# Fillers from the first q piece, a cast load for block 0 of v, and its copies moved to ScalarE in a fused attention and channel-mix kernel

## The chip, the cores and the metric

The kernel runs on one core of a Trainium2 chip. The metric is device time in microseconds (us), as the median of several executions; less is better. PE is TensorE, DVE is VectorE, ACT is ScalarE, POOL is GpSimd; SP issues DMAs. Times on a timeline count from the start of the span. "L148" is line 148 of the kernel that the line is from; the changed kernel's numbers differ by a few. "Warm" and "cold" stand for PE at full and at half pace.

## The reference, cut to what matters

```python
# q, k, v: (4, 6208, 256) fp32
qn = q / (norm(q, axis=1) + 1e-6);  kn = k / (norm(k, axis=1) + 1e-6)
s = kn.transpose(0, 2, 1) @ qn / tau            # (4, 256, 256)
a = softmax(s, axis=-1)
x = v @ a
# channel mix of x with its rows shifted by one
xk = mu_k * x + (1 - mu_k) * x_prev;  xr = mu_r * x + (1 - mu_r) * x_prev
out = sigmoid(xr @ w_r) * (relu(xk @ w_k) ** 2 @ w_v)
```

A batch's `a` needs all rows of its q and k. So the kernel first streams q and k of batch 0 (12.7 MB), finishes its softmax, and only then can start on v. From there it works block by block (512 rows), and does the q and k work of batches 1 to 3 beside the blocks of the batch before.

## The kernel before: the parts concerned

The first stage takes pieces of 512 rows, in the order q q q q q q q, then k and q in turn, then the remaining k. Each piece is loaded as fp32, cast by DVE and squared by ACT; PE adds up `k^T q` in one PSUM bank and the column sums of the squares (128x1 matmuls) in another.

```python
    def q_piece(g, last=False):
        rows, n = rows_of(g)
        f = head_load(q, 0, g, 0, n)                       # SP, fp32
        qt = pq.tile([P, S, C], BF16, name="qb", ...)
        nc.vector.tensor_copy(qt[:rows, :n], f[:rows, :n])
        sq = pq.tile([P, S, C], BF16, name="hsq", tag="hsq", bufs=5)
        nc.scalar.activation(sq[:rows, :n], f[:rows, :n], AF.Square)
        flush()                                            # norm matmuls of the piece before
        pend.append((nq_ps, "q", sq, rows, n, last))
    # ... k_piece: the same, and 8 matmuls of 128x256 into s_ps0
    def filler(n):                                         # work for PE whose result nobody reads
        f_ps = ps.tile([P, M], F32, name="f_ps", tag="v", bufs=2)
        for u in range(n):
            nc.tensor.matmul(f_ps, ident, qb[0]...[:, :M], start=u == 0, stop=u == n - 1)
    # ... in the loop over pieces, after a k piece:
            if g == NB - 3:
                nc.scalar.copy(rq_bc0, bc_ps)              # the q norm, broadcast to all rows
            # ...
            if g == NB - 3:
                nc.gpsimd.tensor_copy(gate, kt[:, 0, 0:1]) # holds POOL until this k piece is cast
                nc.gpsimd.dma_start(w_k_sb, ...)           # cast loads, fp32 to bf16
                v_load(1)
                nc.gpsimd.dma_start(w_r_sb, ...)
                nc.gpsimd.dma_start(w_v_sb, ...)
```

After the last k piece comes the seam: block 0 of v by two plain loads and a cast on ACT, root and reciprocal of the k norm, exp, the scaled `a_sb`, the transposed block 0, the first mixed rows `xk` and the first up-projection `kT_ps`. After that PE is nearly always busy until the end.

Of the kernel before, what the change touches and what calls it, by code (L numbers as in the profile page):

```python
# [10 lines left out]
F32 = mybir.dt.float32  # L11
BF16 = mybir.dt.bfloat16
AX = mybir.AxisListType.X
AF = mybir.ActivationFunctionType
OP = mybir.AluOpType
# [3 lines left out]
def kernel(  # L19
# [13 lines left out]
    nc = tc.nc  # L33
    B, N, C = q.shape
    D = C
    DF = moe_w_k.shape[1]
    P = 128
    M = 512
    S = M // P
    assert C == 256 and DF == 1024  # L40
    NB = N // M
# [9 lines left out]
    pq = ctx.enter_context(tc.tile_pool(name="pq", bufs=4))  # L51
# [6 lines left out]
    ident = const.tile([P, P], BF16, name="ident")  # L58
# [16 lines left out]
    w_v_sb = const.tile([P, 8, D], BF16, name="w_v_sb")  # L75
    w_r_sb = const.tile([P, 2, D], BF16, name="w_r_sb")
    a_sb = const.tile([P, B, 2, C], BF16, name="a_sb")
    rq_bc0 = const.tile([P, C], F32, name="rq_bc0")
# [7 lines left out]
    def rows_of(g):  # L86
        return (P, S) if g < NB else (L, 1)


    qb = {}  # L90
    hk = {}
    NF = 8
    LEAD = 6
    F1, F2, F3 = 8, 2, 4
    NPE = 4

    def head_load(t, b, g, s0, s1):
        rows = rows_of(g)[0]
        f = pq.tile([P, S, C], F32, name="f", tag="f4", bufs=NF)
        nc.sync.dma_start(f[:rows, :s1 - s0], src_rows(t, b, g, s0, s1))  # L100
        return f
# [3 lines left out]
    s_ps0 = ps.tile([P, 2, C], F32, name="s_ps", tag="s")  # L105
    started = set()

    def first(key):
        if key in started:
            return False  # L110
        started.add(key)
        return True
# [9 lines left out]
    def flush():  # L122

        while pend:
            norm_mm(*pend.pop(0))

    def q_piece(g, last=False):
        rows, n = rows_of(g)
        f = head_load(q, 0, g, 0, n)
        qt = pq.tile([P, S, C], BF16, name="qb", tag="b2", bufs=NB + 1)  # L130
        qb[g] = qt
        nc.vector.tensor_copy(qt[:rows, :n], f[:rows, :n])
        sq = pq.tile([P, S, C], BF16, name="hsq", tag="hsq", bufs=5)
        nc.scalar.activation(sq[:rows, :n], f[:rows, :n], AF.Square)
        flush()
        pend.append((nq_ps, "q", sq, rows, n, last))

    def k_piece(g, s0, s1, last=False):
        rows, n = rows_of(g)
        n = s1 - s0  # L140
        f = head_load(k, 0, g, s0, s1)
        kt = pq.tile([P, S, C], BF16, name="kb", tag="kb", bufs=4)
        nc.vector.tensor_copy(kt[:rows, :n], f[:rows, :n])
        sq = pq.tile([P, S, C], BF16, name="hsq", tag="hsq", bufs=5)
        nc.scalar.activation(sq[:rows, :n], f[:rows, :n], AF.Square)
        for s in range(n):
            for ih in range(2):
                nc.tensor.matmul(s_ps0[:, ih, :], kt[:rows, s, ih * P:(ih + 1) * P], qb[g][:rows, s0 + s, :],  # L148
                                 start=first("s"), stop=last and s == n - 1, skip_group_check=True)
        flush()  # L150
        pend.append((nk_ps, "k", sq, rows, n, last))
        return kt

    def root(src, n):
        a = pn.tile([P, 4], F32, name="nrm_a")
        if len(src.shape) == 3:
            nc.vector.tensor_reduce(a[:, :n], src, axis=AX, op=OP.add)
        else:
            nc.vector.tensor_copy(a[:, :n], src)
        r = pn.tile([P, 4], F32, name="nrm_r")  # L160
        nc.gpsimd.tensor_tensor(r[:, :n], a[:, :n], half[:, :n], op=OP.pow)
        return r

    def inverse(r, n):

        nc.vector.tensor_scalar_add(r[:, :n], r[:, :n], 1e-6)
        o = pn.tile([P, 4], F32, name="nrm_o")
        nc.vector.reciprocal(o[:, :n], r[:, :n])
        return o


    def spread(r):
        dq = pn.tile([P, 2, P], F32, name="dq", bufs=1)
        for h in range(2):
            nc.vector.tensor_scalar_mul(dq[:, h], ident_f, r[:, h:h + 1])
        return dq

    def broadcast(dq, tag, **kw):
        bc_ps = ps.tile([P, C], F32, name="bc_ps", tag=tag, **kw)
        nc.tensor.matmul(bc_ps, ones_f, dq.rearrange("p h d -> p (h d)"), start=True, stop=True)  # L180
        return bc_ps

    def filler(n):

        f_ps = ps.tile([P, M], F32, name="f_ps", tag="v", bufs=2)
        for u in range(n):
            nc.tensor.matmul(f_ps, ident, qb[0].rearrange("p s c -> p (s c)")[:, :M], start=u == 0, stop=u == n - 1)

    def soft_half(b, ih, t_sb, rk, e_sb, sm, mx):

# [13 lines left out]
    def soft_tiles():  # L204
        return (pn.tile([P, 2, C], F32, name="t_sb"), pn.tile([P, 2, C], F32, name="e_sb"),
                pn.tile([P, 2], F32, name="sm"), pn.tile([P, 2], F32, name="mx"))
# [7 lines left out]
    st = {}  # L214
# [4 lines left out]
    def v_load(i):  # L219
        b, t = blocks[i]  # L220
        v_bf = pq.tile([P, S, C], BF16, name="v_bf", tag="b2", bufs=NB + 1)
        nc.gpsimd.dma_start(v_bf, v[b, t * M:(t + 1) * M, :].rearrange("(s p) c -> p s c", p=P))  # L222
        st[i, "v"] = v_bf

    def new_vT(i):

        vT = pq.tile([P, S, 2, P], BF16, name="vT", tag="b2", bufs=NB + 1)
        st[i, "vT"] = vT
        return vT
# [6 lines left out]
    def v_transpose_pe(i, v_bf, s0, s1, evac):  # L236
        vT = st[i, "vT"] if (i, "vT") in st else new_vT(i)
        n = s1 - s0
        vT_ps = ps.tile([P, S, 2, P], BF16, name="vT_ps", tag="kT", bufs=3)
        for s in range(n):  # L240
            for h in range(2):
                nc.tensor.transpose(vT_ps[:, s, h], v_bf[:, s0 + s, h * P:(h + 1) * P], ident)
        if evac == "v":
            nc.vector.tensor_copy(vT[:, s0:s1], vT_ps[:, :n])
        else:
            nc.scalar.copy(vT[:, s0:s1], vT_ps[:, :n])
# [263 lines left out]
    for what, g in order:  # L510
        if what == "q":
            q_piece(g, last=g == NB - 1)
        else:
            kt = k_piece(g, 0, rows_of(g)[1])
            if g == NB:
                nq = root(nq_ps, 2)
            if g == NB - LEAD + 1:
                bc_ps = broadcast(spread(inverse(nq, 2)), "v", bufs=2)
            if g == NB - 3:
                nc.scalar.copy(rq_bc0, bc_ps)  # L520
            if g == NB - 2:
                nc.sync.dma_start(mu_k_t, moe_mu_k.rearrange("(h p) -> p h", p=P))
                nc.sync.dma_start(mu_r_t, moe_mu_r.rearrange("(h p) -> p h", p=P))
            if g == NB - 3:
                nc.gpsimd.tensor_copy(gate, kt[:, 0, 0:1])
                nc.gpsimd.dma_start(w_k_sb, moe_w_k.rearrange("(ko ki) f -> ki ko f", ki=P))
                v_load(1)
                nc.gpsimd.dma_start(w_r_sb, moe_w_r.rearrange("(ko ki) d -> ki ko d", ki=P))
                nc.gpsimd.dma_start(w_v_sb, moe_w_v.rearrange("(fo fi) d -> fi fo d", fi=P))
    k_piece(NB - 1, 0, 2)  # L530
    k_piece(NB - 1, 2, 3)
    k_piece(NB - 1, 3, 4, last=True)
    flush()

    f0 = []
    for h in range(2):
        f = pq.tile([P, S, C], F32, name="f", tag="f4", bufs=NF)
        nc.sync.dma_start(f[:, :2], v[0, h * 256:(h + 1) * 256, :].rearrange("(s p) c -> p s c", p=P))
        f0.append(f)
    v0 = pq.tile([P, S, C], BF16, name="v_bf", tag="b2", bufs=NB + 1)  # L540
    for h in range(2):
        nc.scalar.copy(v0[:, 2 * h:2 * h + 2], f0[h][:, :2])

    t_sb, e_sb, sm, mx = soft_tiles()
    rk = root(nk_ps, 2)
    nc.vector.tensor_tensor(t_sb[:, 0], s_ps0[:, 0], rq_bc0, op=OP.mult)
    rk = inverse(rk, 2)
    if inv_tau != 1.0:
        nc.vector.tensor_scalar_mul(rk[:, 0:2], rk[:, 0:2], inv_tau)
    nc.vector.tensor_tensor(t_sb[:, 1], s_ps0[:, 1], rq_bc0, op=OP.mult)  # L550
    for ih in range(2):
        soft_half(0, ih, t_sb, rk, e_sb, sm, mx)
    nc.vector.tensor_scalar(omu, mu_k_t, -1.0, 1.0, op0=OP.mult, op1=OP.add)
    v_load(2)
    pos = {"load": 0}

# [7 lines left out]
    v_load(3)  # L564
    more_rows(3)
    v_load(4)
    for h in range(2):
        v_transpose_pe(0, v0, 2 * h, 2 * h + 2, "v")
    filler(F1)
    for ih in range(2):  # L570
        soft_scale(0, ih, e_sb, sm)

# [15 lines left out]
    for i in range(-2, NBLK):  # L588
        for j in range(8):
# [23 lines left out]
            n = i + 2  # L613
# [21 lines left out]
            if chain and (chain[0] is None or chain[0].__name__ != "bcast" or j in (3, 7)):  # L635
                f = chain.pop(0)
# [9 lines left out]
            for u in due.get(T, []):  # L646
                b, g, s = units[u]
# [48 lines left out]
```

## Time and profile before

| What | Value | Where from |
|---|---|---|
| time | 520.86 us (520.62 to 521.65, 4 runs) | timed runs |
| PE busy | 493.4 of 518.7 us, 95% | page, part 1 |
| last k piece lands | 37.0 us | DMA issues |
| k norm complete | 41.21 us | PE timeline, end of the last nk_ps matmul |
| first up-projection | 47.40 us | PE timeline |
| first full q, k group of batch 1 | lands 51.04, first used 53.45 us | DMA issues, PE timeline |

Read it from the end. PE bounds everything after about 52 us, so only the time up to the first up-projection can be won. The prediction shows the lines.

### The profile page before, as it was taken

What the parts mean: (1) busy time and instruction counts of PE and PEld (TensorE: products, weight loads), DVE (VectorE), ACT (ScalarE), POOL (GpSimd) and SP (SyncE); (2) the same over time, 40 slices, a digit from 0 to 9 for tenths busy, and PEclk for the clock granted to TensorE, in tenths of its full rate; (3) what the DMA queues carried; (4) which work ended last, traced back from release to release, by engine and by line L of the source; (5) the groups of instructions that cost most, each with busy time, mean ns of one, the idle gap of its engine ahead of it and who ended that gap; (6) DMA issues with size and microseconds to landing.
All of it is one profiled execution on the core that took longest, in us unless ns stands there. A gap on an engine that the chain in (4) does not pass through costs nothing. (4 is left out here: it accounts for less than half of the span.)

```text
span 518.7 us, 10189 instructions
## 1 busy us (share of the span) xinstructions
PE 493.4 (95%) x3730; PEld 340.5 (66%) x3730; DVE 451.6 (87%) x896; ACT 434.6 (84%) x831; POOL 102.9 (20%) x144
## 2 busy tenths in 40 slices
PE   1788999999999999999999999999999999999996
PEld 1564576676666667667666767667666666666675
DVE  3456899999999999999999999999988888888884
ACT  5776889998999899899999989899787777777773
POOL 0037432322251131131152123100031000000000
PEclk9999999999999999999999999999999999999999
DMA  8999999999999999699699999944298663432113
GB/s 309 407 329 185 193 204 193 196 204 186 132 185 219 164 169 171 117 175 170 108 168 220 167 170 168 157 114 85 61 163 147 128 117 87 102 83 80 57 66 102
DMA packets 143218, 83.77 MB, mean 161 GB/s; under 512 B 51200, under 2 KB 139840, under 8 KB 143168
## 3 DMA queue, kind: packets, MB, share of 16 engines
q0 software_dynamic: 65280, 32.74, 49.3%
q1 hardware_dynamic: 77728, 50.25, 39.2%
q8 instruction: 29, 0.48, 0.4%
q14 instruction: 21, 0.17, 0.1%
q10 hardware_dynamic: 160, 0.13, 0.1%
HBM read 78.71 MB, written 25.43 MB: 201 GB/s over the span
## 5 line engine op out<-in xcount | busy, mean ns | idle before, releaser
L337 ACT ACTIVATE kr<-kT_ps 128x512 bf16<-128x512 f32 (+1 forms) x392 | 232.4, 595 | 37.6 <-PE kT_ps L334 30.3
L334 PE MATMUL kT_ps<-xk,w_k_sb 128*128 128x512 bf16 (+1 forms) x784 | 231.6, 377 | 1.8 <-DVE xk L319 1.6
L382 PE MATMUL v_ps<-w_v_sb,kk 128*128 128x256 bf16 x1536 | 230.4, 273 | 0.0
L343 DVE TENSOR_TENSOR kk<-kr 128x512 bf16<-128x512 bf16 (+1 forms) x392 | 161.4, 416 | 35.8 <-ACT kr L337 32.2
L382 PEld LDWEIGHTS <-kk 128*128 128x128 bf16 x1536 | 150.2, 98 | 57.6
L425 ACT ACTIVATE sq<-qk 128x512 f32<-128x512 bf16 (+1 forms) x147 | 93.0, 633 | 0.0
L334 PEld LDWEIGHTS <-w_k_sb 128*128 128x128 bf16 x784 | 74.7, 98 | 22.4 <-issue 1.0
L353 PE MATMUL g_ps<-w_r_sb,xr 128*128 128x256 bf16 x388 | 73.8, 272 | 1.1 <-ACT ssq L462 1.1
L255 ACT CAST X<-xT_ps 128x512 bf16<-128x512 f32 x94 | 55.5, 590 | 20.8 <-PE xT_ps L253 20.0
L319 DVE SCALAR_TENSOR_TENSOR xr<-delta,mu_r_t,X 128x512 bf16<-128x512 bf16 x96 | 71.3, 743 | 0.0
L353 PEld LDWEIGHTS <-xr 128*128 128x128 bf16 x388 | 37.9, 98 | 48.9 <-issue 5.7
L319 DVE SCALAR_TENSOR_TENSOR xk<-delta,mu_k_t,X 128x512 bf16<-128x512 bf16 x94 | 69.9, 744 | 0.0
L395 DVE SCALAR_TENSOR_TENSOR res<-res,v_ps 128x512 f32<-128x512 f32 x96 | 65.2, 679 | 0.0
L411 POOL DMA_DIRECT2D qk<-in_q_dram x39 | 28.7, 736 | 170.4 <-ACT sq L425 167.0
L388 ACT ACTIVATE res<-g_ps 128x512 f32<-128x512 f32 x97 | 57.8, 596 | 0.4 <-PE g_ps L353 0.4
L253 PE MATMUL xT_ps<-vT,a_sb 128*128 128x512 bf16 x188 | 55.9, 379 | 0.2 <-ACT X L280 0.2
L421 PE MATMUL s_ps<-qk 128*128 128x256 bf16 (+1 forms) x294 | 56.1, 272 | 0.0
L222 POOL DMA_DIRECT2D v_bf<-in_v_dram x47 | 36.1, 774 | 51.4 <-DMA vT<-v_bf 46.7
L443 DVE TENSOR_TENSOR sq<-sq 128x1024 f32<-128x1024 f32 x36 | 43.8, 1218 | 1.0 <-ACT sq L425 1.0
L421 PEld LDWEIGHTS <-qk 128*128 128x128 bf16 (+1 forms) x294 | 26.7, 97 | 12.4 <-issue 1.3
L308 DVE TENSOR_TENSOR delta<-X 128x1024 bf16<-128x1024 bf16 x48 | 32.9, 685 | 0.1
L411 POOL DMA_DIRECT2D qk<-in_k_dram x39 | 29.0, 743 | 2.3 <-DMA qk<-in_q_dram 1.0
(73 smaller groups left out, 229.5 us busy)
## 6 DMA issues: line engine op xcount, KB each, us to landing
out_dram<-res SPq DMA_DIRECT2D x48, 512.0 KB, 3.4
v_bf<-in_v_dram POOLq DMA_DIRECT2D x47, 256.0 KB, 7.9
qk<-in_q_dram POOLq DMA_DIRECT2D x36, 256.0 KB, 6.6
qk<-in_k_dram POOLq DMA_DIRECT2D x36, 256.0 KB, 7.8
f<-in_q_dram SPq DMA_DIRECT2D x12, 512.0 KB, 8.6
f<-in_k_dram SPq DMA_DIRECT2D x11, 512.0 KB, 9.1
vT<-v_bf SPq DMA_TRANSPOSE x44, 6.5
f<-in_v_dram SPq DMA_DIRECT2D x2, 256.0 KB, 4.8
```

Source lines behind the costliest of these rows:

```text
L253: nc.tensor.matmul(xT_ps, a_sb[:, b, ih, dh * P:(dh + 1) * P], vT[:, :, ih, :], start=ih == 0, stop=ih == 1)
L319: nc.vector.scalar_tensor_tensor(o[:, dh], st[i, "d"][:, dh], mu[:, dh:dh + 1], X[:, dh, c:c + M], op0=OP.mult, op1=OP.add)
L334: nc.tensor.matmul(kT_ps[:, :m], w_k_sb[:, dh, fh * P:(fh + 1) * P], xk[:, dh, :m], start=dh == 0, stop=dh == 1)
L337: nc.scalar.activation(kr[:, :m], kT_ps[:, :m], AF.Relu, scale=RH)
L343: nc.vector.tensor_tensor(st[i, "kk"][:, fh, :m], kr[:, :m], kr[:, :m], op=OP.mult)
L353: nc.tensor.matmul(g_ps[:, s % 2], xr[:, dh, s * P:(s + 1) * P], w_r_sb[:, dh, :], start=s % 2 == 0 and dh == 0, stop=dh == 1, skip_group_ ...
L382: nc.tensor.matmul(v_ps[:, s % 2], kk[:, fh, s * P:(s + 1) * P], w_v_sb[:, fh, :], start=s % 2 == 0 and fh == 0, stop=fh == 7, skip_group_ ...
L388: nc.scalar.activation(st[i, "res"][:, 2 * u:2 * u + 2], st.pop((i, "g", u)), AF.Tanh, scale=0.5)
L395: nc.vector.scalar_tensor_tensor(r, r, 1.0, st.pop((i, "v", u)), op0=OP.add, op1=OP.mult)
L411: nc.gpsimd.dma_start(qk[:rows, :n, i], src_rows(t, b, g))
L421: nc.tensor.matmul(cov[b][:, ih, :], qk[:rows, s, 1, ih * P:(ih + 1) * P], qk[:rows, s, 0, :], start=g == GORD[0] and s == 0 and ih == 0, ...
L425: nc.scalar.activation(G["sq", s // 2][:rows, s % 2], qk[:rows, s], AF.Square)
```

## The change

The intent: keep PE busy from the start so that it runs at full pace when the last k pieces arrive; take ACT's wait for the q norm row away; spare ACT the cast of block 0; and free DVE in the seam. In the diff below, cuts are marked with "...".

```diff
-    F1, F2, F3 = 8, 2, 4
+    F1, F2, F3, FQ = 12, 2, 4, 3
...  in q_piece
         pend.append((nq_ps, "q", sq, rows, n, last))
+        if g < NB:
+            filler(FQ, g)
...  in k_piece
-        kt = pq.tile([P, S, C], BF16, name="kb", tag="kb", bufs=4)
+        kt = pq.tile([P, S, C], BF16, name="kb", tag="kb", bufs=6)
...  filler(n, src=0) reads qb[src] instead of qb[0]
-            if g == NB - 3:
-                nc.scalar.copy(rq_bc0, bc_ps)
+            if g == NB - 2:
+                nc.vector.tensor_copy(rq_bc0, bc_ps)
...
                 nc.gpsimd.tensor_copy(gate, kt[:, 0, 0:1])
+                v_load(0)
                 nc.gpsimd.dma_start(w_k_sb, ...)
                 v_load(1)
-                nc.gpsimd.dma_start(w_r_sb, ...)
-                nc.gpsimd.dma_start(w_v_sb, ...)
...  two plain loads of block 0 of v and their casts on ACT: taken out
+    v0 = st.pop((0, "v"))
+    for h in range(2):
+        v_transpose_pe(0, v0, 2 * h, 2 * h + 2, "s")      # copied from PSUM by ACT
+    filler(F1)
     for ih in range(2):
         soft_half(0, ih, t_sb, rk, e_sb, sm, mx)
...  both halves of t_sb are now made ahead of the reciprocal (one was behind it)
+    nc.gpsimd.dma_start(w_r_sb, ...)
+    nc.gpsimd.dma_start(w_v_sb, ...)
     v_load(2)
...
-    for h in range(2):
-        v_transpose_pe(0, v0, 2 * h, 2 * h + 2, "v")      # copied by DVE, after exp
-    filler(F1)
```

More of the change, by code (lines that the diff above doesn't have):

```diff
@@ L181, in broadcast, with filler @@
         return bc_ps
-    def filler(n):
+    def filler(n, src=0):
         f_ps = ps.tile([P, M], F32, name="f_ps", tag="v", bufs=2)
         for u in range(n):
-            nc.tensor.matmul(f_ps, ident, qb[0].rearrange("p s c -> p (s c)")[:, :M], start=u == 0, stop=u == n - 1)
+            nc.tensor.matmul(f_ps, ident, qb[src].rearrange("p s c -> p (s c)")[:, :M], start=u == 0, stop=u == n - 1)
     def soft_half(b, ih, t_sb, rk, e_sb, sm, mx):
@@ L525 @@
                 nc.gpsimd.tensor_copy(gate, kt[:, 0, 0:1])
+                v_load(0)
                 nc.gpsimd.dma_start(w_k_sb, moe_w_k.rearrange("(ko ki) f -> ki ko f", ki=P))
                 v_load(1)
-                nc.gpsimd.dma_start(w_r_sb, moe_w_r.rearrange("(ko ki) d -> ki ko d", ki=P))
-                nc.gpsimd.dma_start(w_v_sb, moe_w_v.rearrange("(fo fi) d -> fi fo d", fi=P))
     k_piece(NB - 1, 0, 2)
@@ L533 @@
     flush()
-    f0 = []
-    for h in range(2):
-        f = pq.tile([P, S, C], F32, name="f", tag="f4", bufs=NF)
-        nc.sync.dma_start(f[:, :2], v[0, h * 256:(h + 1) * 256, :].rearrange("(s p) c -> p s c", p=P))
-        f0.append(f)
-    v0 = pq.tile([P, S, C], BF16, name="v_bf", tag="b2", bufs=NB + 1)
-    for h in range(2):
-        nc.scalar.copy(v0[:, 2 * h:2 * h + 2], f0[h][:, :2])
     t_sb, e_sb, sm, mx = soft_tiles()
     rk = root(nk_ps, 2)
-    nc.vector.tensor_tensor(t_sb[:, 0], s_ps0[:, 0], rq_bc0, op=OP.mult)
+    for ih in range(2):
+        nc.vector.tensor_tensor(t_sb[:, ih], s_ps0[:, ih], rq_bc0, op=OP.mult)
     rk = inverse(rk, 2)
@@ L549 @@
         nc.vector.tensor_scalar_mul(rk[:, 0:2], rk[:, 0:2], inv_tau)
-    nc.vector.tensor_tensor(t_sb[:, 1], s_ps0[:, 1], rq_bc0, op=OP.mult)
+    v0 = st.pop((0, "v"))
+    for h in range(2):
+        v_transpose_pe(0, v0, 2 * h, 2 * h + 2, "s")
+    filler(F1)
     for ih in range(2):
@@ L553 @@
     nc.vector.tensor_scalar(omu, mu_k_t, -1.0, 1.0, op0=OP.mult, op1=OP.add)
+    nc.gpsimd.dma_start(w_r_sb, moe_w_r.rearrange("(ko ki) d -> ki ko d", ki=P))
+    nc.gpsimd.dma_start(w_v_sb, moe_w_v.rearrange("(fo fi) d -> fi fo d", fi=P))
     v_load(2)
@@ L566 @@
     v_load(4)
-    for h in range(2):
-        v_transpose_pe(0, v0, 2 * h, 2 * h + 2, "v")
-    filler(F1)
     for ih in range(2):
```

## The prediction

> **What bounds the kernel now.** I read the page first (parts 1 and 2), then the timelines of PE, ACT, DVE and POOL from 0 to 60 us, then the DMA issues of that stretch with their times to landing.
>
> ```profile
> PE 493.4 (95%) x3730; PEld 340.5 (66%) x3730; DVE 451.6 (87%) x896; ACT 434.6 (84%) x831; POOL 102.9 (20%) x144
> PE   1788999999999999999999999999999999999996
> ```
>
> From slice 5 on (about 52 us) PE is busy nine tenths or more and the change touches nothing there. So the change can only move the moment at which that PE-bound run starts. Before it lie two stages: about 37 us in which q and k of batch 0 stream in through fp32 tiles, and a "seam" of about 10 us (key norm, softmax, first v block, first mixed rows) up to the first up-projection, at 47.40 us. The seam, on the PE timeline:
>
> ```profile
> 32.26 1.89 PE L148 MATMUL s_ps<-qb,kb 128*128 128x256 bf16 x8 [0.87 <-DVE kb L143]
> 34.22 1.80 PE L148 MATMUL s_ps<-qb,kb 128*128 128x256 bf16 x8
> 36.06 0.68 PE L180 MATMUL bc_ps<-dq,ones_f 128*128 128x256 f32 x2
> 36.57 1.04 PE L148 MATMUL s_ps<-qb,kb 128*128 128x256 bf16 x8
> 37.65 1.03 PE L148 MATMUL s_ps<-qb,kb 128*128 128x256 bf16 x8
> ...
> 40.97 0.24 PE L117 MATMUL nk_ps<-ones_b,hsq 128*128 128x1 bf16 x4
> ...
> 45.00 0.39 PE L268 MATMUL xT_ps<-vT,a_sb 128*128 128x512 bf16 x1 [0.38 <-DVE a_sb L202]
> ...
> 47.40 0.85 PE L334 MATMUL kT_ps<-xk,w_k_sb 128*128 128x512 bf16 x2
> ```
>
> Columns: start, duration, engine, line, operation. The same eight matmuls take 1.89 us, then 1.04. Taking off one matmul (0.42 and 0.27 us) and dividing by 7 gives 0.21 and 0.11 us from start to start: PE is at half pace until about 36 us. From 32.26 on, no line of PE shows an idle wait until after 43 us: it works off a backlog. The last k piece lands at 37.0 us (issued at 31.55, 5.5 us to landing), yet the key norm is complete only at 41.21 (40.97 + 0.24). ACT loses time as well:
>
> ```profile
> 36.77 0.37 ACT L520 COPY rq_bc<-bc_ps 128x256 f32<-128x256 f32 x1 [1.56 <-PE bc_ps L180]
> 37.04 2.32 ACT L145 ACTIVATE hsq<-f 128x1024 bf16<-128x1024 f32 x4
> 39.27 1.12 ACT L542 CAST v_bf<-f 128x512 bf16<-128x512 f32 x2
> 42.64 0.51 ACT L197 ACTIVATE e_sb<-t_sb,nrm_o 128x256 f32<-128x256 f32 x1 [2.25 <-DVE nrm_o L168]
> ```
>
> It stands 1.56 us for the broadcast of the q norm, which waits its turn behind cold matmuls on PE, and the last four squares therefore end at 39.36.
>
> **What the Trainium skill says.** (1) "TensorE: Matmul & The Clock Gate", Part 1: the array idles at 1.2 GHz and goes to 2.4 GHz after about 3.4 us of sustained work; "Wait — 56ns, not 53.3ns?" there gives N / 1.2 GHz cold and N / 2.4 GHz + 2.5 ns warm, that is 213 and 109 ns for N = 256. The trace agrees on both paces, and PE had worked without a gap for 3.6 us (32.26 to about 35.85) when the pace changed. From 14 to 24 us PE had gaps of only 0.26 us in each 2.55 and stayed cold. The page's PEclk row shows 9 throughout and does not tell the two apart. (2) Same page, "Why this matters for your kernels": no idle gaps over about 3 us. Between 43.4 and 47.4 us gaps of 0.8 and 0.4 us left it warm. (3) "DMA: Bandwidth & Descriptors", "Issuing engines are not separate DMA queues": loads issued by SP and GpSimd share the same 16 engines. In the trace, cast loads move about 190 GB/s in bf16 bytes, which is 380 GB/s of fp32 read, against 400 to 420 for plain loads: a cast load is no cheaper on the engines, it only takes the cast off ACT.
>
> **The change, part by part.**
>
> *Fillers after each of 12 q pieces, 3 of N = 512.* Cold they cost 3 x 0.427 = 1.28 us (pace as above, scaled to 512), with the eight norm matmuls 0.37 us: 1.65 us of work per 1.28 us piece. PE saturates from about 6 us and should be warm by 10 to 13 us. Warm, a pair of a q and a k piece needs 7 x 0.11 + 0.27 = 1.04 (s) + about 0.55 (norms) + 0.65 (fillers) = 2.2 us per 2.55 us of loading, so there is no backlog. Fillers end with the last q piece (28.8 us); k pieces alone then cost about 1.07 us each (37.65 less 36.57) per 1.28 us, 80%, which I expect to keep PE warm. PE is not the bound there, so 36 fillers add nothing directly. The first stage stays bound by DMA: the last k piece still lands at 37.0.
>
> *q norm row copied by DVE, two pieces later.* Takes away ACT's 1.56 us wait and 0.27 us of copy (37.04 less 36.77). The square of k piece 10 starts at its landing, 35.55, and the four squares end at 35.55 + 2.32 = 37.9; DVE pays 0.37 us among its casts.
>
> *kb buffers 4 to 6.* Removes two DVE waits for PE (0.58 and 0.83 us before the last two casts), which a PE without backlog would have removed anyway.
>
> *Norm complete:* 37.9 + last four norm matmuls, about 0.35 = **38.3** instead of 41.21: 2.9 us earlier.
>
> *Chain from norm to exp.* Before: copy 41.24, power on POOL to 42.20, reciprocal to 42.6, exp at 42.64, that is 1.43 us after the norm. After: the same, 39.75, if ACT is free. But v of block 0 now comes by a cast load, issued behind the gate (k piece 9, 35.0 before), and its two transposed halves are copied on ACT ahead of exp. The first cast load's packets begin to move about 2 us after issue, as k ends; 256 KB at 190 GB/s is 1.35 us, so it lands at about 38.7. Transposes to 39.2, two ACT copies of about 0.55 us from 39.1: exp starts at about **40.3**, not 39.75. DVE, rid of the vT copies (0.75 us), then scales sooner: before, the second a_sb let PE go 2.36 us after exp began (45.00 less 42.64); I take 1.9. So xT at 42.2 against 45.00: **2.8 us** gained. F1 = 12 fillers (2.6 us from 39.2) end at 41.8, just before.
>
> *After it* the steps to the first up-projection are unchanged (2.4 us), so 44.6 instead of 47.40. Block 1 of v (landed 42.3) is needed at about 43.3, w_k (landed 40.95) at 44.6. w_r and w_v are issued later but fall in behind v1 in a queue that never empties; they are needed after 51. Load order and bytes are otherwise the same, so landings hardly move.
>
> Sum: 520.77 - 2.8 = **518.0 us**.
>
> **Rivals.** *(a) The cast load is the new bound.* v of block 0 gates both ACT copies and, through ACT's order, exp. For: its issue waits for the gate and the first packets of this queue are slow (171 GB/s from 36 to 38 us). Against: the estimate above leaves it 0.5 us late only. If it lands at 40 instead of 38.7, gain 1.5 us: 519.3. *(b) The loop becomes load-bound.* The first full q, k group lands at 51.04 (k part: issued 44.78, 6.3 us) and was first used at 53.45, a slack of 2.41 us, less than the 2.8 gained; the next groups have 5.6 us and more. So PE may wait 0.4 us once; but DVE is 97% busy from 48 to 58 and PE waits on it there anyway (0.60 us before 54.78), so I count 0.1 us. If it cascades: 519.5. *(c) PE stays or falls cold again* in the k-only stretch: the backlog returns and the norm is back at about 40.5 to 41; gain 0 to 0.7: 520.3. *(d) Nothing reaches the end.* A shift of the start under a PE bound passes through whole; I see no later stop.
>
> **Range and chances.** Centre 518.0; (a) to (c) all push up, a faster seam (exp not held by ACT) would give 517.4. Eight in ten: 517.0 to 519.9. Two per cent is 10.4 us, the whole seam: faster by that 0.01, slower 0.01, same 0.98.
>
> **What would show it.** s_ps groups of eight at 1.04 us from the first k piece on; ACT without the wait for bc_ps; last nk_ps matmul ending at 38.3; first v load landing at 38.7 and exp at 40.3; first kT at 44.6; PE's wait before the first full group under 0.5 us; PE busy time over the span about unchanged. The prediction is wrong if 8-matmul groups near 36 us still take 1.89, if exp waits on v well past 40.3, or if kT starts early but the end does not follow.

## The result, and the profile after

The changed kernel takes **518.88 us** (518.72 to 519.07, 4 runs) against 520.86: 2.0 us less. The ratio is 0.9960, 95% interval 0.9942 to 0.9977. A repeat later, in 5 rounds, gave 518.88 us again and a ratio of 0.9967 (0.9955 to 0.9979). That is within the range of 517.0 to 519.9, and short of the centre, 518.0, by 0.9 us.

The page of the changed kernel, parts 1 and 2:

```profile
PE 496.5 (96%) x3770; PEld 340.4 (66%) x3770; DVE 451.2 (87%) x895; ACT 434.7 (84%) x830; POOL 104.1 (20%) x145
PE   5789899999999999999999999999999999999996
```

The first slices of PE are fuller (5, 7, 8, 9 instead of 1, 7, 8, 8): those are the fillers. The fifth is emptier than its neighbours, 8; that is the new thing to explain. The PE timeline of the changed kernel (start, duration, engine, line, operation, count, and in brackets the idle time before it and what ended it):

```profile
6.16 1.44 PE L189 MATMUL f_ps<-qb,ident 128*128 128x512 bf16 x3 [2.56 <-DVE qb L132]
...
9.14 1.30 PE L189 MATMUL f_ps<-qb,ident 128*128 128x512 bf16 x3
...
10.48 0.81 PE L189 MATMUL f_ps<-qb,ident 128*128 128x512 bf16 x3
...
13.85 1.05 PE L150 MATMUL s_ps<-qb,kb 128*128 128x256 bf16 x8 [0.46 <-DVE kb L145]
...
31.80 1.05 PE L150 MATMUL s_ps<-qb,kb 128*128 128x256 bf16 x8 [0.87 <-DVE kb L145]
...
38.91 0.24 PE L117 MATMUL nk_ps<-ones_b,hsq 128*128 128x1 bf16 x4
39.58 0.62 PE L244 MATMUL vT_ps<-ident,v_bf 128*128 128x128 bf16 x8 [0.43 <-DMA v_bf<-in_v_dram]
...
42.63 0.59 PE L270 MATMUL xT_ps<-vT,a_sb 128*128 128x512 bf16 x2
...
45.48 0.60 PE L336 MATMUL kT_ps<-xk,w_k_sb 128*128 128x512 bf16 x2
...
50.54 0.39 PE L423 MATMUL s_ps<-qk 64*128 64x256 bf16 x2 [0.39 <-DMA qk<-in_k_dram]
...
53.21 0.39 PE L423 MATMUL s_ps<-qk 128*128 128x256 bf16 x2 [1.29 <-DMA qk<-in_k_dram]
```

Three fillers take 1.44 us at first and 0.81 us from 10.5 us on: PE has reached full pace, 25 us sooner than before, and in this trace every k group of eight matmuls takes 1.03 to 1.05 us. The k norm is complete at 39.15 us (38.91 + 0.24) instead of 41.21, and the first up-projection starts at 45.48 instead of 47.40: 1.92 us sooner. Then come two waits that the kernel before did not have. In the waits of PE between 46 and 150 us (who waited for whom: us in total, times, longest), the largest of each kernel are, before and then after:

```profile
PE kT_ps L334 <- DVE xk L319: 0.6, 1, 0.6
```
```profile
PE s_ps L423 <- DMA qk<-in_k_dram: 1.7, 2, 1.3
```

Lining up the up-projection matmuls of both traces one by one gives the gain along the way: 1.91 us at the first, 2.16 at the fifth, 0.35 at the seventeenth (just after the second wait), 1.30 at the nineteenth, and 1.25 at the last of 784. So about 0.9 us of the 2.16 was given back within 9 us, and the rest went through to the end unchanged. (In this pair of traces the spans differ by 1.4 us, 518.7 and 517.3; the timed medians by 2.0.)

ACT in the seam of the changed kernel:

```profile
35.49 2.19 ACT L147 ACTIVATE hsq<-f 128x1024 bf16<-128x1024 f32 x4 [0.30 <-DMA f<-in_k_dram]
40.01 1.07 ACT L248 COPY vT<-vT_ps 128x512 bf16<-128x512 bf16 x2 [2.33 <-PE vT_ps L244]
40.97 0.52 ACT L199 ACTIVATE e_sb<-t_sb,nrm_o 128x256 f32<-128x256 f32 x1
```

The wait for the q norm row is gone and the last squares end at 37.68 us. But exp (L199) starts at 40.97, right behind the two vT copies, and these waited 2.33 us for the transposes, which wait for block 0 of v: it lands at 39.53 us (issued 35.06, on its way for 4.5 us).

### The profile page after: what moved, and what is told of

The parts are those of the page before. It is cut to its first block, busy times and chain, and to the rows that moved or that the text cites. A ratio compares the mean times of both kernels' runs of the same rounds, so it can differ in the third digit from the quotient of the medians.

```text
span 517.3 us, 10260 instructions
## 1 busy us (share of the span) xinstructions
PE 496.5 (96%) x3770; PEld 340.4 (66%) x3770; DVE 451.2 (87%) x895; ACT 434.7 (84%) x830; POOL 104.1 (20%) x145
## 5 line engine op out<-in xcount | busy, mean ns | idle before, releaser
L355 PEld LDWEIGHTS <-xr 128*128 128x128 bf16 x388 | 37.9, 98 | 48.2 <-issue 4.8
L224 POOL DMA_DIRECT2D v_bf<-in_v_dram x48 | 37.3, 779 | 52.4 <-DMA vT<-v_bf 46.9
```

The lines of the kernel that those rows point to most:

```text
L355: nc.tensor.matmul(g_ps[:, s % 2], xr[:, dh, s * P:(s + 1) * P], w_r_sb[:, dh, :], start=s % 2 == 0 and dh == 0, stop=dh == 1, skip_group_ ...
```

## The experiments

Two questions were open. Which part of the change won the 2 us at the start? Theory A says the warm PE; its rival, the parts that relieve ACT and DVE. And what made the loop's loads late? Theory B says the cast load of block 0, theory C (formed after theory B's runs) that together with the late issue of w_r and w_v. Theory D, on what bounds the tail of k, came last. Twelve runs were made, two of them repeats, all correct, with 5 rounds each. For each, from its trace: the end of the last nk_ps matmul ("norm"), the start of the first up-projection ("up"), the landing of the first full q, k group of batch 1 ("group"), and PE's waits for qk in sum.

| Run | median us | ratio to before | norm | up | group | waits |
|---|---|---|---|---|---|---|
| before | 520.86 | 1 | 41.21 | 47.40 | 51.04 | 0 |
| changed | 518.88 | 0.9960 | 39.15 | 45.48 | 53.16 | 1.7 |
| no_fill | 521.90 | 1.0013 | 42.00 | 47.93 | 55.45 | 1.3 |
| fill_only | 518.61 | 0.9949 | 39.03 | 45.22 | 50.50 | 0 |
| v0_plain | 518.96 | 0.9955 | 39.17 | 45.11 | 52.92 | 1.6 |
| gate_early | 519.32 | 0.9968 | 39.37 | 45.62 | 53.40 | 1.8 |
| w_early | 518.60 | 0.9952 | 39.20 | 45.59 | 52.79 | 1.0 |
| loads_back | 518.01 | 0.9942 | 38.96 | 44.53 | 50.66 | 0 |
| fill_root | 518.41 | 0.9950 | 38.93 | 45.11 | 50.83 | 0 |
| fill_six | 520.97 | 1.0003 | 41.54 | 47.72 | 51.64 | 0 |
| after_again | 518.88 | 0.9967 | 39.24 | 45.74 | 53.15 | 1.3 |
| back_again | 517.81 | 0.9946 | 39.07 | 44.64 | 50.90 | 0 |
| back_kb4_rq | 517.69 | 0.9945 | 39.41 | 44.98 | 50.71 | 0 |
| loads_root | 517.62 | 0.9941 | 38.94 | 44.51 | 50.55 | 0 |

The ratios' intervals are about 0.0012 to either side (0.0018 for the first result); the last four columns come from one trace each, and the two traces of the changed kernel differ by 0.26 us in "up" and 0.4 us in the waits; "before" of the table is the first measurement, and each group of four had its own runs of it (medians 521.35, 521.18 and 520.76).

### no_fill and fill_only: the fillers alone

no_fill is the changed kernel without them; fill_only is the kernel before with nothing else.

```diff
 no_fill
-        if g < NB:
-            filler(FQ, g)
 fill_only (on the kernel before)
+        if g < NB:
+            filler(FQ, g)
```

> The changed kernel without the three fillers after each q piece. Theory A (warm PE shortens the tail of k): the s_ps groups of eight take 1.89 us again up to about 36 us, the last nk_ps matmul ends at 40.5 to 41.2 instead of 39.15, first kT at about 47, total 520.0 to 520.8 us. Rival (the copy on VectorE and the other v path did it, the fillers are idle work): nk_ps still ends before 39.5 and the total stays within 0.4 us of 518.9.

> The kernel before plus only the fillers of the q pieces (F1 stays 8, v by plain loads, q norm row copied on ScalarE). Theory A: nk_ps ends at about 39.2, first kT at about 45.5, and because the loads land as before (first full q, k group at 51.0) PE waits for it less than 0.5 us: total 518.5 to 519.0, as good as the whole change or better. Rival: 520.3 to 520.8.

The PE timeline of no_fill:

```profile
18.95 1.05 PE L148 MATMUL s_ps<-qb,kb 128*128 128x256 bf16 x8 [0.64 <-DVE kb L143]
...
21.50 1.89 PE L148 MATMUL s_ps<-qb,kb 128*128 128x256 bf16 x8 [1.13 <-DVE kb L143]
...
36.84 1.56 PE L148 MATMUL s_ps<-qb,kb 128*128 128x256 bf16 x8
...
41.76 0.24 PE L117 MATMUL nk_ps<-ones_b,hsq 128*128 128x1 bf16 x4
```

and that of fill_only, with ACT's copy of the q norm row last:

```profile
32.79 1.05 PE L150 MATMUL s_ps<-qb,kb 128*128 128x256 bf16 x8
...
38.79 0.24 PE L117 MATMUL nk_ps<-ones_b,hsq 128*128 128x1 bf16 x4
...
45.22 0.85 PE L336 MATMUL kT_ps<-xk,w_k_sb 128*128 128x512 bf16 x2
```
```profile
35.17 0.35 ACT L522 COPY rq_bc<-bc_ps 128x256 f32<-128x256 f32 x1
```

Without fillers the norm is complete at 42.00 us and nothing is gained; the total is even a little over the kernel before (521.90 against 521.35 in the same rounds). The norm, the first up-projection and the total all came later than expected. PE did reach full pace by itself, at 17.42 us, but fell back at 20.83 and stayed at half pace until 37.90 us, within the group at 36.84: about 2 us later than in the trace of the kernel before (35.80). With fillers alone it is complete at 39.03 us, the first up-projection starts 2.18 us sooner than before, and the lined-up gain is still 2.17 us at the last one: all of it arrives. So the fillers alone give the whole gain of the change; what its other parts win and lose comes below. fill_only's ACT also copies the q norm row without any wait (at 35.17, right behind the square before): ACT's 1.56 us of before were PE's slow pace, seen from ACT.

### fill_six: is it enough to warm PE up once?

```diff
 fill_six (on fill_only)
-        if g < NB:
+        if g < LEAD:            # LEAD = 6
             filler(FQ, g)
```

> Fillers alone on the kernel before, but only after the first six q pieces; none after 13 us. If fillers are needed only to warm PE and its own work (some 60 per cent of a q, k pair) holds it: s_ps groups of eight stay at 1.05 us throughout, total 518.6 as with all twelve. Rival (the own work lets it fall back as it never warmed it up): groups go back to 1.89 us before 30 us, total 520.3 to 521.

The PE timeline of fill_six:

```profile
21.51 1.05 PE L150 MATMUL s_ps<-qb,kb 128*128 128x256 bf16 x8 [1.13 <-DVE kb L145]
...
25.42 1.89 PE L150 MATMUL s_ps<-qb,kb 128*128 128x256 bf16 x8 [2.48 <-DVE kb L145]
```

The expectation fell, but not at once. PE's own work held the full pace through four k groups with idle waits of up to 1.18 us. The next group, after a wait of 2.48 us, is at half pace. There the loads paused: 2.5 us pass between two landings, 20.74 and 23.26, instead of the usual 1.28 (the kernel before has the same pause, 2.25 us from 21.04 on). The total, 520.97, is that of the kernel before.

That the long wait took the pace is not shown, though. Here is the busy time by stretch in fill_six (stretch; its length; busy us of PE, PEld, DVE, ACT and POOL; granted clock; DMA share; GB/s):

```profile
22.00:23.00 1.00, 0.94 (x22) 0.80 (x19) 0.00 (x0) 0.00 (x0) 0.00 (x0) 1.00 1.04 414
23.00:24.00 1.00, 0.00 (x0) 0.00 (x0) 0.69 (x1) 0.64 (x1) 0.00 (x0) 0.51 1.01 401
```

The granted clock fell at 23.03 us, when the wait had lasted 0.1 us. In no_fill it fell at 20.83, after a wait of 0.64 us and 0.5 us into one of 1.13. And three runs with all twelve groups of fillers lost the pace too, v0_plain at 22.87, loads_root at 23.14 and back_kb4_rq at 24.70 us, with waits of 1.73 to 1.95 us in the same pause of the loads. They had it back 3.4 us later, as v0_plain's PE timeline shows:

```profile
22.86 1.89 PE L150 MATMUL s_ps<-qb,kb 128*128 128x256 bf16 x8 [1.73 <-DVE kb L145]
...
26.25 1.06 PE L150 MATMUL s_ps<-qb,kb 128*128 128x256 bf16 x8
```

In each of these five traces the recorded changes before 40 us lie whole multiples of 3.41 us apart (3.41, 13.65 and 17.07 us). What decides at such a moment stays open: PE was busy for 43% (loads_root) to 68% (no_fill) of the 3.41 us before a fall, and for only 56% before a moment of fill_six, 16.20 us, without one. What the runs do show is the outcome. With twelve groups of fillers PE was at full pace from 28.2 us on in every trace, in time for the tail of k; without the last six it came back only at 36.68 us. The mean granted clock of the timed runs agrees: 0.994 or more in every run with twelve groups, 0.980 to 0.986 in all five of fill_six, and below 0.990 in 20 of the 31 runs of the kernel before that ran beside the experiments. By this, most runs of the kernel before reached full pace early and lost it again; its profiled run, at half pace until 35.80 us, is not typical in that.

### v0_plain, gate_early, w_early, loads_back: why the loads are late

In the changed kernel three things differ in the loads: block 0 of v goes through the cast queue, no plain load runs while that queue starts up, and w_r and w_v are issued only after the k norm.

```diff
 v0_plain   (on the changed kernel): block 0 of v by two plain loads on SP, cast on ACT
-                v_load(0)
+    # after the last k piece, as in the kernel before
 gate_early (on the changed kernel)
-            if g == NB - 3:
+            if g == NB - 4:
                 nc.gpsimd.tensor_copy(gate, kt[:, 0, 0:1])
 w_early    (on the changed kernel): w_r and w_v behind the gate again, no longer after the k norm
                 v_load(1)
+                nc.gpsimd.dma_start(w_r_sb, ...)
+                nc.gpsimd.dma_start(w_v_sb, ...)
 loads_back: v0_plain and w_early together
```

> The changed kernel, but block 0 of v comes as in the kernel before, by two plain fp32 loads on SP and a cast on ScalarE. Theory B (the cast load of v0 is what delays the later cast loads: it replaces a transfer that filled the DMA engines while the first cast load was being set up): the first full q, k group lands at about 51.0 to 51.5 instead of 53.16, PE's waits for qk fall from 1.7 us to under 0.7, total 517.9 to 518.3. Rival (the late issue of w_r and w_v delays them): the waits stay above 1.2 us and the total stays at 518.9.

> The changed kernel with the gate of the cast loads at the k piece before (NB - 4 instead of NB - 3), about 1.2 us earlier. Theory B: the DMA engines' hole between 35 and 37.5 us closes in part, v0 lands at about 38.3 instead of 39.53, the first full q, k group at about 52.0 instead of 53.16, PE's waits for qk fall to about 0.5 us, total 517.9 to 518.3. Rival (the early cast loads take bandwidth from the last k pieces): last k lands 0.5 to 1 us later than 36.77 and the total stays within 0.3 us of 518.9.

> The changed kernel with w_r and w_v issued again behind the gate, right after block 1 of v. Theory C (two holes in the DMA stream push the loop's loads back: one of 2 us before the first cast load, since no plain v load fills it, and one that comes of issuing w_r and w_v only after the key norm): the second hole goes and the first stays, the first full q, k group lands at 51.8 to 52.4 instead of 53.16, PE waits 0.7 to 1.3 us for it instead of 1.7, first kT stays at 45.5, total 518.2 to 518.6. Rival (only the first hole counts): still 53.1 and 518.9.

> The changed kernel with all its loads as in the kernel before: block 0 of v by two plain loads and a cast on ScalarE, w_r and w_v behind the gate. Fillers, 6 kb buffers, q norm row on VectorE, vT copied on ScalarE and 12 fillers in the seam stay. Theory C: first full q, k group lands at about 51, PE waits for it under 0.7 us, first kT gains 2.3 us and all or nearly all of it arrives at the end: total 518.3 to 518.7, the same as fillers alone within 0.3 us. Rival (something else in the new parts costs time in the loop): 518.9 or more.

The busy times by stretch, in the columns of above, tell where the DMA engines had little to do. First the changed kernel, then v0_plain, then loads_back:

```profile
36.00:38.00 2.00, 2.00 (x33) 1.82 (x32) 1.46 (x5) 1.68 (x4) 1.92 (x3) 1.00 0.37 49
42.00:44.00 2.00, 2.00 (x10) 0.76 (x8) 0.64 (x4) 0.76 (x2) 2.00 (x4) 1.00 1.40 192
```
```profile
36.00:38.00 2.00, 2.00 (x33) 1.82 (x32) 1.45 (x5) 2.00 (x5) 0.68 (x1) 1.00 0.85 156
42.00:44.00 2.00, 1.74 (x12) 0.75 (x11) 0.80 (x3) 0.69 (x2) 2.00 (x4) 1.00 0.83 97
```
```profile
36.00:38.00 2.00, 2.00 (x34) 1.82 (x32) 1.47 (x5) 2.00 (x5) 2.00 (x3) 1.00 1.07 166
42.00:44.00 2.00, 2.00 (x17) 1.15 (x16) 0.80 (x3) 1.26 (x2) 1.88 (x3) 1.00 1.45 202
```

In the changed kernel the engines move 49 GB/s from 36 to 38 us, since the k loads are done and the cast queue has only begun; with the plain loads of v they move 156. From 34 to 38 us the plain loads make up 0.5 MB, all of block 0 in fp32, in time that is otherwise lost; cast, the same block takes 256 KB / 190 GB/s = 1.4 us of the queue that everything later waits in. In v0_plain that hole is filled and another opens, 97 GB/s from 42 to 44 us: with less ahead of them, the late w_r and w_v now find the queue run dry. In loads_back neither is there, the first full group lands at 50.66, and PE does not wait.

Theory B fell with v0_plain: it expected the group by 51.5, waits under 0.7 and 518.3 us or less, and got 52.92, 1.6 and 518.96. Theory C had the two costs add up, and that part was wrong: w_early was expected to land the group by 52.4, and landed it at 52.79. Against loads_back (50.66) each of the two alone costs about 2 us at that group, both together 2.5. A likely reason is that a queue pushed back by the one still has work when the other's hole would come: in the changed kernel 192 GB/s move from 42 to 44 us. How much of the cast load's cost is the lost time and how much its own 1.4 us in the queue was not separated. gate_early, which was to close the first hole in part, missed too: the gate came only about 0.6 us sooner in this trace (issue at 34.44 instead of 35.06), v0 landed at 38.99, the last k piece was late by 0.27 us (37.04), and the second hole (120 GB/s from 43 to 44 us) ate the rest; 519.32 us is no better than the changed kernel.

loads_back is faster than both kernels, 518.01 us, and faster than was expected (518.3 to 518.7): its first up-projection starts 2.87 us sooner than before, not 2.3. Run again beside the changed kernel:

> The changed kernel once more, as the yardstick of the next three on the same chip: 518.7 to 519.2 us, PE's waits for qk 1.5 to 1.8 us in sum.

> The changed kernel with its loads as in the kernel before, once more beside the changed kernel. Theory C: 0.6 to 1.2 us faster than the changed kernel of the same rounds, ratios apart by 0.0012 to 0.0023. If the first result was chance: within 0.3 us.

517.81 against 518.88 us, ratios 0.9946 and 0.9967: 1.1 us, as expected (the changed kernel's waits were 1.3 us this time, under the expected 1.5 to 1.8). Its first up-projection starts at 44.53 us (44.64 in the repeat), 0.6 to 0.7 us ahead of fill_only's 45.22, though the norm ends within 0.1 us of it. That is what the rest of the change is worth in the seam, with the vT copies on ACT and DVE free to scale at once; its parts (these copies, 12 fillers instead of 8, the order of the t_sb products) were not tested apart. In the timed runs the difference of loads_back and fill_only (0.9946 or 0.9942 against 0.9949, in different rounds) is within the intervals, so it is seen in the traces alone.

### back_kb4_rq: the kb buffers and the q norm row

```diff
 back_kb4_rq (on loads_back)
-        kt = ... bufs=6
+        kt = ... bufs=4
-            if g == NB - 2:
-                nc.vector.tensor_copy(rq_bc0, bc_ps)
+            if g == NB - 3:
+                nc.scalar.copy(rq_bc0, bc_ps)
```

> The same with 4 kb buffers and the q norm row copied on ScalarE at its old place. If these two parts only removed waits that a warm PE removes anyway: within 0.3 us of that kernel, ScalarE's copy of 0.35 us without a wait of over 0.2 us, VectorE without waits for PE before its last casts. Rival (each is worth its wait of before, 1.56 us and 1.41 us): the last nk_ps matmul ends 0.5 us or more later and the total is 518.5 to 519.5.

517.69 against 517.81 us of the same rounds. ACT's copy takes 0.35 us without a wait, and DVE waits for PE before none of its last casts. The norm ends 0.34 us later than in back_again, inside what was allowed. The two parts, taken back together, buy nothing measurable: both waits were PE's pace.

### fill_root and loads_root: what bounds the tail of k now

In the warm runs so far DVE stands 1.3 to 1.5 us for the q norm before it casts k piece 6, already landed. These two take the norm one piece later.

```diff
 fill_root (on fill_only), loads_root (on loads_back)
-            if g == NB:
+            if g == NB - LEAD:
                 nq = root(nq_ps, 2)
```

> Fillers alone on the kernel before, and the root of the q norm taken one k piece later in VectorE's order, so that the cast of k piece 6, landed at 30.2 us, need not stand behind the wait for the q norm (1.33 us in the trace). Theory D (with a warm PE the tail of k is bound by PE from the first of its k pieces on, 31.7 us): PE starts that tail 0.7 us sooner, the last nk_ps matmul ends at 38.1 to 38.5 instead of 39.0, total 517.9 to 518.2 against 518.6 of fillers alone. Rival (ScalarE's squares or the landings bound the tail): unchanged within 0.3 us.

> The changed kernel with its loads as before and the root of the q norm one k piece later. The tail of k is then bound by the landings (fill_root ended nk_ps only 0.1 us sooner): within 0.3 us of the kernel without the moved root, and PE's first full group waits for its load up to 0.3 us. If PE's late start was the bound after all: 0.5 us faster.

In fill_root PE starts k piece 6 at 31.07 instead of 31.68 us, and yet the norm ends at 38.93 instead of 39.03: PE now waits for a cast of k piece 10 (0.20 us, before 36.43) and then runs without a gap:

```profile
36.43 1.05 PE L150 MATMUL s_ps<-qb,kb 128*128 128x256 bf16 x8 [0.20 <-DVE kb L145]
...
38.69 0.24 PE L117 MATMUL nk_ps<-ones_b,hsq 128*128 128x1 bf16 x4
```

Theory D fell (it expected the norm by 38.5 and 518.2 us or less; the total is 518.41). Its rival had the right size, within 0.3 us, but only half the reason: the landing and cast of piece 10 set the start, and what remains is PE's own work from there, 2.5 us from 36.43. loads_root, 517.62 us, is 0.2 us under back_again, within the noise, as expected; PE did not wait for its first full group. It is the fastest median by a hair; the simpler loads_back is as good within the intervals.

## Why the prediction was right or wrong

**Warm PE: right.** Predicted by 10 to 13 us, seen at about 10.3; k groups at 1.05 us from the first on; no backlog at the end of the q pieces. That fillers after the last q piece are not needed also held. In part this was luck: "I expect to keep PE warm" rested on 80% load (1.07 of 1.28 us is 84%), and neither the load nor the wait alone sorts the traces that lost the pace, with all fillers in three of them, from those that kept it.

**Norm complete at 38.3: too early by 0.85 us.** The failed step is "37.9 + last four norm matmuls, about 0.35". ACT's squares did end when predicted (37.68), but PE was not waiting for them: from 31.80 us it has no idle wait until 39.15, and 1.47 us of its own work was left when ACT was done. Six k pieces at 1.07 us, the last of them in three parts, and the broadcast, about 0.5 us, fill that time. I compared PE's 1.07 us with the 1.28 us of a landing and concluded that there was no backlog. I left out that after piece 10 is cast PE still has two pieces to do, 2.5 us in fill_root. That PE gets k piece 6 only at 31.80 (landed 30.2) adds little: fill_root starts it 0.6 us sooner and gains 0.1 us. Measured gain of this term 2.06 us, predicted 2.9.

**The 1.56 us of ACT and the kb waits: listed as gains of their own, not so.** The prediction said of the buffers that a warm PE would remove their waits anyway, and back_kb4_rq shows it; the same is true of ACT's wait, which the prediction booked to the copy on DVE. (The copy moved by one k piece, from NB - 3 to NB - 2, not by two as the prediction says.)

**v of block 0: right in kind.** Rival (a) was partly there: landing at 39.53 instead of 38.7, exp at 40.97 instead of 40.3. POOL spent 1.35 us on the first cast load's issue, and its first packets moved between 37.0 and 37.5 us, about 2 us after the issue began. "DMA: Bandwidth & Descriptors" in the Trainium skill, section "Anatomy of one DMA", gives about 2.0 us fixed cost for a DMA of this path and puts most of it after the last byte. This trace has a cost of that size, but elsewhere: the 2 us lie before the first packet, and the landing came about 0.3 us after the queue had moved the block's 256 KB (39.24). From exp to the second product of xT I took 1.9 us, and that was right: the pair runs from 42.63, its second matmul from 42.84, 1.87 after exp (up to 0.2 us of it behind the 12 fillers: the second a_sb is ready at 42.65).

**"Load order and bytes are otherwise the same, so landings hardly move": wrong.** This is the other step that failed. The bytes are the same only if fp32 and cast loads count alike. The plain load used engines that were otherwise idle; the cast load came first in the queue that all later loads wait in. And "in a queue that never empties" was read off the kernel before, where w_r and w_v were issued early; v0_plain, at 97 GB/s from 42 to 44 us, shows the hole. The first full group landed 2.1 us later (53.16, not 51.04). Rival (b) named the right group and the right margin, 2.41 us, but kept the landing fixed and priced the wait at 0.1 us; it cost about 0.9.

**Pass-through: right.** After the loads had caught up the gain stayed at 1.30 to 1.25 us to the end, and in fill_only at 2.17. The sum 2.8 us was thus 2.1 at the norm, 1.9 to 2.2 at the up-projection and, less 0.9 in the loop, 1.3 in the traces; the timed medians give 2.0. The total lies in the range because that left 1.9 us above the centre, not because this wait was foreseen.

## What to carry to other kernels

Waits on other engines can all be one engine's slow pace: make that engine fast first, alone, and see what is left of the list. In this load-bound stage 36 filler matmuls cost nothing measurable; those of its first half alone warmed PE up but did not hold the pace, so follow the pace in the trace to the end of the stage. When a stage is pulled forward, check the margin of each load behind it, and count a moved load on the queue that it joins, not by its bytes.

## What the Trainium skill lacked or had wrong

- "TensorE: Matmul & The Clock Gate", "Why this matters for your kernels": it allows idle gaps up to about 3 us. Here the pace was lost with shorter ones: in fill_six 0.1 us into a wait of 2.48 us, in no_fill 0.5 us into one of 1.13 us, in v0_plain at the end of one of 1.73 us. Waits of 1.13 to 1.18 us in fill_six had not lost it. (Another section of the page knows of a pace lost to frequent short gaps, but gives no length.)
- The same page, Part 1: it asks for about 3.4 us of sustained work. It does not say how dense: matmuls with idle waits of 0.23 to 0.26 us in each 2.55 us stayed at half pace from 14 to 24 us in the kernel before, while in no_fill the pace rose at 17.42 us in spite of a wait of 0.25 us.
- Beyond a general caveat on recorded clock events in that Part 1, no page says how a profile's clock row reads before the first recorded change. Here it reads full: 9 in every slice of the kernel before, though eight matmuls took 1.89 us in one part and 1.04 in another. In no_fill a group of 1.89 us at 13.86 us stands at 1.00, and one of 1.89 us at 21.50, after a recorded fall, at 0.50.
- "DMA: Bandwidth & Descriptors" has no figure for casting loads: here about 190 GB/s counted in bf16, 380 in fp32, and 1.35 us of POOL for the issue of the first (0.73 to 0.79 us for the next two). Its "Anatomy of one DMA" puts most of the fixed 2.0 us after the last byte; for block 0 of v 2 us passed before the first packet and 0.3 us after the last.
